# Moving two casts, one weight load, one transpose and two low parts in a mixed linear-attention and expert kernel

## The chip, the core and the metric

The kernel runs on one core of one Trainium2 chip. The metric is the device time of one execution in microseconds (us); lower is better. Engines are named as the profile names them: PE multiplies matrices, DVE, ACT and POOL work on tiles element by element, SP issues most DMAs. All work in their own order and wait for one another through semaphores.

## What is computed

Each of 2048 rows of x (512 wide) goes through two branches, and a gate mixes them.

```python
qkv = x @ wqkv                                    # q, k, v: 32 heads of 16
phi(a) = concat(softmax(a @ w_phi), softmax(-a @ w_phi))
kv, z  = sum_s phi(k) v, sum_s phi(k)             # over all rows
A = (phi(q) @ kv) / (phi(q) @ z + 1e-6) @ wo
q1, q2 = halves of x @ w_q                        # 32 heads
e = argmax(q1 @ k1.T) * 16 + argmax(q2 @ k2.T)    # one of 256 experts per head
B = sum over heads of gelu(x . u[e]) * v[e]
g = sigmoid(x . gate_w);  out = g * A + (1 - g) * B
```

## The kernel before

Rows are cut into 16 tiles of 128. To keep precision, an operand of a product is held as a high part (a cast, names ending in h) and a low part (the value minus the cast, names ending in l), and a product is three matmuls: high by high, high by low, low by high. A matmul over 512 columns is the unit in what follows.

**First phase (tiles 0 to 15).** Keys and values of a tile are projected, the softmaxes of the keys are made (`k_diffs` on DVE, `k_exp` on ACT, `k_sum` on DVE, `k_mult` on POOL), and `kvacc` adds the products with the values in one PSUM bank. From tile 5 on, tiles go in pairs (t, t+1) by a scheme that needs sums of the two tiles: `Sums.add` builds them on POOL, `Sums.high` casts them on ACT into `gh` (first sum) and the `xh` of tile 15's place (second sum), `Sums.low` subtracts on POOL into `gl` and `xl`. The products of a pair go into four rotating PSUM banks named pk, pu, pv and pk; a bank that is copied from another one is first written by ACT (L482: pu from pk), and pu of the next pair takes the bank of pv of this pair, which DVE's L549 reads last.

Beside this, the expert scores' weights are folded: `score` multiplies a piece of w_q (16 pieces, `load_wq` brings them into two buffers) with the keys k1, k2; `score_planes` (L297 on ACT, then a transposing DMA on SP) turns the result by way of 16-bit planes; `join_tp` and `join_end` (L308, L314 on ACT, L315 on POOL) put the planes together and split them into `sh`, `sl`. At t = 13 the query weights `rawq` come into one of the same two buffers, and PE folds them with w_phi (`foldq`, L208).

**Second phase (a = 0 to 15).** In step a the tile a is at the queries' softmax, b = a - 1 at turning and joining its planes, z = a - 2 at the output product. For tile z the products run: `mid_num` (L765, from `pt`, the joined planes of tile z's attention weights), the casts `xh` of its result (L769, ACT), the low parts `xl` (`num_lo`, L776, DVE), `back` (L877: 12 matmuls with `wo`'s parts; L884: 6 matmuls with `ch`, `cl`, the expert coefficients of the tile), `store`. The coefficients come from `count` (a chain of small bit operations on DVE, which `step` and `drain` deal out between other work; L800 to L824), `coef` (L828 on POOL), `c_planes` (L833 on ACT, a transposing DMA on SP), `c_join` (L840, L844 on ACT), `back_cl` (L865, DVE). `best` (L722, L723 on DVE) finds the best expert half by half, `turn_eq` sends its result through a transposing DMA on SP.

`wo` has four pieces. Pieces 2 and 3 are loaded together into one tile (`rawo2`, in the pool `late`); their high parts are made on ACT (L944, L973) and the low parts on POOL: piece 2 (`gl`) at L945 ahead of the loop, piece 3 (`wbl`) at L988 in step 1. After that `late` is closed (`cl_.close()` in step 1) and the pool `w4` is opened in the same memory; `pt` is its first tile, so the first `join` (L756) must wait until the last reader of `rawo2` has finished.

Nothing is scheduled automatically: each engine gets its instructions in the order in which the code issues them, and a wait holds up all that stands behind it on that engine. SP's DMAs are issued in order too.

Of the kernel before, what the change touches and what calls it, by code (L numbers as in the profile page):

```python
# [16 lines left out]
ALU = mybir.AluOpType  # L17
# [3 lines left out]
P = 128  # L21
S = 2048
D = 512
NT = S // P
# [11 lines left out]
def mix_kernel(ctx, tc, xT, wqT, wkT, wv, wphi, wo, wq, kk, ug, ev, cst, out):  # L36
# [103 lines left out]
    def stage(src, name, shape=None):  # L140
        t_ = wa_.tile(shape or [P, NK, D], F32, tag="st", bufs=2, name=name)
        if src is not None:
            sp.dma_start(t_, src)
        return t_
# [121 lines left out]
    def k_exp(t):  # L266
        act.activation(phis[t], phis[t], AF.Exp)  # L267
# [39 lines left out]
    def join_tp(j, tp, tj):  # L307
        act.copy(tj.bitcast(U16).rearrange("p (k n j) -> p j k n", j=2, n=P),  # L308
                 tp.rearrange("p (j k) n -> p j k n", j=2))

    def join_end(j, tj):
        js = slice(P * j, P * j + P)
        t3 = tj.rearrange("p (k e) -> p k e", k=NK)
        act.copy(sh[:, :, js], t3)  # L314
        pool.tensor_tensor(sl[:, :, js], t3, sh[:, :, js], op=ALU.subtract)  # L315

    st8 = {t: {} for t in range(NT)}

# [73 lines left out]
    def score(n, planes=True):  # L392
        nonlocal done
        for _ in range(n):
            score_w(done, raws[done])
            done += 1
            if done < 5:
                load_wq()
            if planes and done % 2 == 0:
                score_planes(done // 2 - 1)  # L400
# [63 lines left out]
    for t in range(5, NT - 1, 2):  # L464
# [53 lines left out]
        if behind:  # L518
            k_exp(behind)
            k_sum(behind)  # L520
            k_mult(behind)
        score(2, t > 5)
        if t > 5:
            load_wq()
            load_wq()
        if t == NT - 3:
            rawq = stage(wqT, "rawq")
        for u in (t - 3, t - 2):
            kvacc(u)
        vn, vt = v_tile(n), v_tile(t)  # L530
# [5 lines left out]
        d = pks[n] = mm_bank(f"pk{n}")  # L536
        act.copy(d, b)
        if t == 5:
            join_end(j2, tj2)
            score_planes(3)  # L540
            k_exp(t)
            x_low(9)
            k_sum(t)
            Sums.high(7, (0,))
            act.copy(vn, by16(e))
        prod(c, sums(1, 2), b22, False)
        if t == NT - 3:
            x_split(NT - 1)
        dve.tensor_tensor(vt, by16(c), vn, op=ALU.add)  # L549
# [1 line left out]
        o2 = d.rearrange("p (c n) -> p c n", c=2)  # L551
        prod(o2, tile_of(n, 2), b4, False)
        if t + 3 < NT:
            Sums.high(t + 2, (0, 1) if t > 5 else (1,))
            Sums.low(t + 2)
        if t == 7:
            for i in range(2):
                x_parts(i, 11)
# [383 lines left out]
        dve.tensor_tensor(zl[i], zsum[:, s_], zh[i], op=ALU.subtract)  # L942
    soft_exp(0)
    act.copy(woh[2], rawo[2])  # L944
    pool.tensor_tensor(wol[2], rawo[2], woh[2], op=ALU.subtract)  # L945
    front_s(1, 0)
    mid_mask(0)
    z_final(zh, zl)
# [12 lines left out]
    for a in range(NT - 1):  # L961
        n, b, z = a + 1, a - 1, a - 2
        owed = min(18, 3 * max(0, a - DEFER))
        left = min(18, 3 * max(0, a - DEFER + 1))
        B, Z = b >= 0, z >= 0
        if Z:
            mid_num(z)
        if a == 2:
            gelu_pre(a)
        if a == 1:  # L970
            front_q(a)
            v15 = vproj(NT - 1)
            act.copy(woh[3], rawo[3])  # L973
        if B:
            planes(b, 0)
            if Z:
                c_join(z)
            if a == 1:
                v15()
            planes(b, 1)  # L980
        if a > 1:
            front_q(a)
        if owed:
            back(z - 1, owed)
            store(z - 1)
        gelu_in(a)
        if a == 1:
            pool.tensor_tensor(wol[3], rawo[3], woh[3], op=ALU.subtract)  # L988
        if Z:
            num_lo(z)  # L990
        if B:
            if a == 1:
                for _ in gate(a):
                    pass
                soft_in(a)
                step(b, 6)
            else:
                soft_in(a, dealt(a, b, z))
                drain(b)
        else:  # L1000
            for _ in gate(a):
                pass
        if a != 1:
            gelu_act(a)
        if a > 0:
            soft_exp(a)
        if Z and not left:
            back(z)
            store(z)
        if not left and a > 1:  # L1010
            mid_mask(a)
        if a:
            front_s(n, 0)
        if left or a == 1:
            mid_mask(a)
            if 0 < left < 18:
                back(z, 18 - left)
        if a == 1:
            kvacc(NT - 1)
            kv_final()  # L1020
            cl_.close()
            w4 = ctx.enter_context(tc_pool("w4", "right"))
        front_s(n, 1)
        front_p(n, False)
        soft_w(a)
        if a == 1:
            best(n, 0)
        soft_sum(a, 0)
        soft_sum(a, 1)
        if a == 1:  # L1030
            drain(b)
        if a == 0:
            step(a, 6)
        if a != 1:
            best(n, 0)
        if a == 0:
            best(n, 1)
            turn_eq(n)
        soft_y(a, 0)
        soft_y(a, 1)  # L1040
        soft_p(a)
        if B:
            join(b)
            gelu_out(b)
            coef(b)
            c_planes(b)
            if a == 1:
                gelu_act(a)
        if a == 0:
            soft_b(a, lambda t: None)  # L1050
        else:
            soft_b(a)
            best(n, 1)
            turn_eq(n)
        if a != 1:
            gelu_pre(n)
# [123 lines left out]
```

## Time and profile before

| | |
|---|---|
| device time, median of 3 runs | 380.41 us (378.58 to 380.72) |
| the profiled execution: its own time | 380.69 us |
| its span, first to last instruction | 378.9 us |
| mean granted clock of PE | 0.991 |
| busy: PE, DVE, ACT, POOL | 97%, 89%, 68%, 54% of the span |

A row of the timeline reads: start in us from the span's first instruction, duration in us, engine, line, operation, output and inputs, shapes, count; then, in brackets, how long the engine sat idle before it and which instruction ended that. A row of windows gives, for a stretch of time, how long each engine was busy (with the number of instructions), and then the mean clock that PE was granted (1.00 is full), the share of DMA time and GB/s.

### The profile page before, as it was taken

The numbers are of one execution on the slowest core, as the hardware profiler recorded it, in microseconds if no ns is written. First come the engines' busy times: TensorE is split into PE (matmuls) and PEld (weight loads), VectorE is DVE, ScalarE is ACT, GpSimd is POOL, SyncE is SP. The second block draws the span as 40 slices with busy tenths as digits, with TensorE's granted clock in tenths as the row PEclk, the third lists the DMA queues.
The fourth block names the chain that finished last, engine by engine and source line by source line (L and its number), as shares of the span: only waits on it lengthen the run. The fifth ranks groups of instructions, "written<-read, shape, count | busy, mean of one in ns | idle before, by whom it ended". The sixth has DMA issues, their size and how long they took to land.

```text
span 378.9 us, 8840 instructions
## 1 busy us (share of the span) xinstructions
PE 367.3 (97%) x3443; PEld 288.0 (76%) x3443; DVE 335.8 (89%) x785; ACT 256.7 (68%) x459; POOL 205.0 (54%) x206
## 2 busy tenths in 40 slices
PE   7999999999999999699999999999999999999995
PEld 4766766877777878578888888888788888888875
DVE  4679999989695989999999999999999999999993
ACT  5576678776554775478768677686696687687741
POOL 1089989978658565336427336344454464364700
PEclk9999999999998999989999999999999999999999
DMA  7867997656852306143361441441643523623501
GB/s 274 325 243 243 285 285 176 213 143 261 304 153 76 84 4 67 20 97 78 77 99 50 104 97 45 83 102 37 113 45 82 126 54 73 126 52 75 69 33 55
DMA packets 72074, 46.67 MB, mean 123 GB/s; under 512 B 63584, under 2 KB 64480, under 8 KB 69728
## 3 DMA queue, kind: packets, MB, share of 16 engines
q1 hardware_dynamic: 71168, 45.24, 45.9%
q10 hardware_dynamic: 864, 0.87, 0.8%
q8 instruction: 27, 0.44, 0.5%
q14 instruction: 15, 0.12, 0.1%
HBM read 26.43 MB, written 4.19 MB: 81 GB/s over the span
## 4 chain that ended last, share of the span: by engine, by line
PE 78%; DVE 9%; POOL 4%; ACT 3%; issue 3%; DMA 2%; POOLq 0%; ACTq 0%
PE po L877 11%; PE s L56 6%; PE s L57 6%; PE s L58 6%; PE pk L454 5%; PE po L884 5%; PE pu L454 4%; PE ws L292 4%; PE pq L56 4%; PE pq L58 3%; PE pq L57 3%; PE oT L765 2%; PE kvacc L283 2%; PE pe L454 2%; PE pv L454 2%
## 5 line engine op out<-in xcount | busy, mean ns | idle before, releaser
L679 POOL TENSOR_TENSOR w<-d,zb 128x512 f32<-128x512 f32 x32 | 41.1, 1302 | 76.1 <-ACT d L673 76.1
L56 PE MATMUL s<-sh,xh 128*128 128x512 f32 x128 | 51.6, 403 | 0.0
L58 PE MATMUL s<-sh,xl 128*128 128x512 f32 x128 | 50.5, 395 | 0.0
L57 PE MATMUL s<-sl,xh 128*128 128x512 f32 x128 | 50.4, 394 | 0.0
L714 POOL TENSOR_TENSOR d<-d,st 128x512 f32<-128x512 f32 x30 | 31.2, 1062 | 30.9 <-DVE st L708 26.6
L673 ACT ACTIVATE d<-d 128x512 f32<-128x512 f32 x32 | 20.0, 632 | 34.0 <-DVE d L119 25.9
L276 POOL TENSOR_TENSOR d<-d,st 128x1024 f32<-128x1024 f32 x16 | 32.5, 2032 | 9.8 <-ACT d L267 7.9
L756 ACT COPY pt<-tp 128x1024 uint16<-128x1024 uint16 x28 | 36.3, 1368 | 0.0
L746 ACT COPY pl<-d 128x1024 uint16<-128x1024 uint16 x28 | 29.2, 1044 | 6.5 <-POOL d L714 6.4
L58 PEld LDWEIGHTS s<-sh,xl 128*128 128x128 f32 x128 | 24.4, 191 | 5.2
L57 PEld LDWEIGHTS s<-sl,xh 128*128 128x128 f32 x128 | 24.5, 191 | 4.8
L56 PEld LDWEIGHTS s<-sh,xh 128*128 128x128 f32 x128 | 24.4, 190 | 4.8
L56 PE MATMUL pq<-wah,xh 128*128 128x512 f32 x64 | 26.8, 418 | 0.0
L58 PE MATMUL pq<-wah,xl 128*128 128x512 f32 x64 | 25.1, 392 | 0.0
L57 PE MATMUL pq<-wal,xh 128*128 128x512 f32 x64 | 25.0, 390 | 0.0
L723 DVE TENSOR_TENSOR eq<-s,mx 128x512 bf16<-128x512 f32 x32 | 22.1, 692 | 1.1
L683 DVE TENSOR_REDUCE st<-d 128x32 f32<-128x512 f32 x32 | 21.6, 681 | 1.4
L722 DVE TENSOR_REDUCE mx<-s 128x32 f32<-128x512 f32 x32 | 21.8, 680 | 0.0
L156 DVE TENSOR_TENSOR xl<-xr,xh 128x512 fp32r<-128x512 f32 (+2 forms) x17 | 20.2, 1204 | 1.7 <-ACT xh L152 1.6
L271 DVE TENSOR_REDUCE st<-d 128x64 f32<-128x1024 f32 x16 | 19.4, 1215 | 2.1 <-ACT d L267 1.8
L693 DVE TENSOR_REDUCE st<-w 128x32 f32<-128x512 f32 x32 | 20.4, 676 | 0.1
L267 ACT ACTIVATE d<-d 128x1024 f32<-128x1024 f32 x16 | 17.1, 1066 | 4.1 <-DVE d L121 4.1
(272 smaller groups left out, 1126.5 us busy)
## 6 DMA issues: line engine op xcount, KB each, us to landing
wq<-wq SPq DMA_DIRECT2D x16, 1024.0 KB, 6.1
xr<-xT SPq DMA_DIRECT2D x15, 256.0 KB, 5.3
y<-ot SPq DMA_DIRECT2D x15, 256.0 KB, 2.3
rawk<-wkT SPq DMA_DIRECT2D x1, 1024.0 KB, 6.1
rawq<-wqT SPq DMA_DIRECT2D x1, 1024.0 KB, 5.4
rawu<-ug SPq DMA_DIRECT2D x2, 258.0 KB, 5.7
rawv<-wv ACTq DMA_DIRECT2D x2, 256.0 KB, 4.5
rawv<-wv SPq DMA_DIRECT2D x2, 256.0 KB, 5.5
```

What stands on the lines that cost most here:

```text
L56: pe.matmul(o, ah, bh, start=(first and i == 0), stop=False)
L57: pe.matmul(o, ah, bl, start=False, stop=False)
L58: pe.matmul(o, al, bh, start=False, stop=(last and i == n - 1))
L276: pool.tensor_tensor(g64(d), g64(d), b64(st[:, 128:192]), op=ALU.mult)
L454: pe.matmul(o, x_, w_, start=(first and i + j == 0), stop=(i == 1 and j == 2), skip_group_check=True)
L679: pool.tensor_tensor(hs(e["w"], i), hs(e["ph"], i), hs(zb, i), op=ALU.mult)
L714: eng.tensor_tensor(g64(d)[:, gs_], g64(d)[:, gs_], r[:, gs_].unsqueeze(2).to_broadcast([P, 32, F]), op=ALU.mult)
L722: dve.tensor_reduce(mx, p3, axis=AX.X, op=ALU.max)
L723: dve.tensor_tensor(e["eq"][:, 512 * half:512 * half + 512].rearrange("p (h f) -> p h f", f=F), p3, mx.unsqueeze(2).to_broadcast([P, H, F] ...
L746: act.copy(pl, e["ph"][:, halves[i]].bitcast(U16).rearrange("p (c j) -> p j c", j=2))
L756: act.copy(p16[:, :, 4 * i:4 * i + 4, :], e["tp"][i].rearrange("p (j g) n -> p j g n", j=2))
L877: pe.matmul(po, a, b, start=(i == 0), stop=False)
```

## The change

Five things are moved; PE's own order stays as it was. (1) At t = 5, ACT casts the first sum of the pair 7, 8 ahead of the exponentials of tile 5, and the second ahead of the copy of tile 6's values; POOL makes both low parts ahead of the low part of the joined scores. (2) At t = 13, the DMA of `rawq` is issued ahead of the transposing DMA of the last scores. (3) Tile 0's coefficient planes (`c_planes(0)`) are made in step 2 behind the casts of tile 0's numerators, no longer in step 1. (4) Piece 2 of `wo` gets its low part in step 0 behind `soft_w`, and piece 3 gets it on DVE, behind `drain(0)` in step 1. (5) Step 0 deals out five of `count`'s pieces for tile 0, not six; the sixth (L800, L802) goes to step 1.

```diff
+    def join_high(j, tj):
+        act.copy(sh[:, :, P * j:P * j + P], tj.rearrange("p (k e) -> p k e", k=NK))
+
+    def join_low(j, tj):
+        js = slice(P * j, P * j + P)
+        pool.tensor_tensor(sl[:, :, js], tj.rearrange("p (k e) -> p k e", k=NK), sh[:, :, js], op=ALU.subtract)
+
     def join_end(j, tj):
...
+        join_high(j, tj)
+        join_low(j, tj)
...
-        score(2, t > 5)
-        if t > 5:
+        score(2, 5 < t < NT - 3)
+        if t == NT - 3:
+            rawq = stage(wqT, "rawq")
+            score_planes(7)
+        elif t > 5:
             load_wq()
             load_wq()
-        if t == NT - 3:
-            rawq = stage(wqT, "rawq")
...
         if t == 5:
-            join_end(j2, tj2)
+            join_high(j2, tj2)
             score_planes(3)
+            Sums.high(7, (0,))
             k_exp(t)
             x_low(9)
             k_sum(t)
-            Sums.high(7, (0,))
+        prod(c, sums(1, 2), b22, False)
+        if t == 5:
+            Sums.high(7, (1,))
             act.copy(vn, by16(e))
-        prod(c, sums(1, 2), b22, False)
...
         if t + 3 < NT:
-            Sums.high(t + 2, (0, 1) if t > 5 else (1,))
+            if t > 5:
+                Sums.high(t + 2)
             Sums.low(t + 2)
+            if t == 5:
+                join_low(j2, tj2)
...
     act.copy(woh[2], rawo[2])
-    pool.tensor_tensor(wol[2], rawo[2], woh[2], op=ALU.subtract)
...
         if a == 2:
+            c_planes(z)
             gelu_pre(a)
...
-        if a == 1:
-            pool.tensor_tensor(wol[3], rawo[3], woh[3], op=ALU.subtract)
...
         if a == 1:
             drain(b)
+            dve.tensor_tensor(wol[3], rawo[3], woh[3], op=ALU.subtract)
         if a == 0:
-            step(a, 6)
+            pool.tensor_tensor(wol[2], rawo[2], woh[2], op=ALU.subtract)
+            step(a, 5)
...
             coef(b)
-            c_planes(b)
             if a == 1:
                 gelu_act(a)
+            else:
+                c_planes(b)
```

Lines of the changed program have other numbers than those of before; the names of the tiles tell which is which. On ACT at t = 5, from the copy into pk of tile 6 to the copy into pu of tile 7, before (xr_397 and xr_359 are the two sums of the pair 7, 8, d_635 tile 5's differences, v_714 tile 6's values):

```order
L537 COPY pk_724<-pu_589 128x512 [waits PE_49]
L314 CAST sh<-wtj_627 128x4x128 [waits Activation_49]
L297 COPY wpl_728<-ws_641 128x1024
L267 ACTIVATE d_635<-d_635 128x1024 [waits DVE_49]
L183 CAST gh<-xr_397 128x512 [waits Pool_49]
L545 COPY v_714<-pe_607 128x32x16
L183 CAST xh_67<-xr_359 128x512 [waits PE_49,Pool_49]
L152 CAST xh_65<-xr_579 128x512 [waits DMAHW5_49]
L482 COPY pu_775<-pk_768 128x512 [waits DVE_49,PE_49]
```

and in the changed program:

```order
L543 COPY pk_724<-pu_589 128x512 [waits PE_49]
L312 CAST sh<-wtj_627 128x4x128 [waits Activation_49]
L297 COPY wpl_727<-ws_641 128x1024
L183 CAST gh<-xr_397 128x512 [waits Pool_49]
L267 ACTIVATE d_635<-d_635 128x1024 [waits DVE_49]
L183 CAST xh_67<-xr_359 128x512 [waits PE_49,Pool_49]
L554 COPY v_714<-pe_607 128x32x16
L152 CAST xh_65<-xr_579 128x512 [waits DMAHW5_49]
L487 COPY pu_775<-pk_768 128x512 [waits DVE_49,PE_49]
```

The cast into gh now stands ahead of the exponentials of tile 5, and the cast into xh_67 ahead of tile 6's values; the copy into pu_775 at the end still waits for DVE.

On ACT in steps 1 and 2, from the copies that join tile 0's planes (pt) to the casts of tile 0's numerators (oT) and the first work of tile 2 (pp), before:

```order
L756 COPY pt_2062<-tp_0_1930 128x2x512 [waits DMAHW3_49,Pool_49]
L756 COPY pt_2062<-tp_0_1935 128x2x512 [waits DMAHW4_49]
L833 COPY plc_2067<-cf_2057 128x512 [waits Pool_49]
L645 ACTIVATE gs_1892<-gs_1892 128x1
L646 ACTIVATE x_1896<-x_1896 128x256
L647 ACTIVATE x_1896<-x_1896,gs_1892 128x256 [waits Activation_49]
L769 CAST xh_65<-oT_0_2091 128x256 [waits PE_49]
L769 CAST xh_65<-oT_0_2092 128x256 [waits PE_49]
L619 ACTIVATE gs_2111<-pp_2031 128x1
```

and in the changed program:

```order
L767 COPY pt_2062<-tp_0_1926 128x2x512 [waits DMAHW3_49,DVE_49,Activation_49]
L767 COPY pt_2062<-tp_0_1931 128x2x512 [waits DMAHW4_49]
L656 ACTIVATE gs_1888<-gs_1888 128x1
L657 ACTIVATE x_1892<-x_1892 128x256 [waits Pool_49]
L658 ACTIVATE x_1892<-x_1892,gs_1888 128x256 [waits Activation_49]
L780 CAST xh_65<-oT_0_2087 128x256 [waits PE_49]
L780 CAST xh_65<-oT_0_2088 128x256 [waits PE_49]
L844 COPY plc_2107<-cf_2056 128x512 [waits Pool_49]
L630 ACTIVATE gs_2111<-pp_2029 128x1
```

The copy of the coefficient planes (plc) has gone behind the casts of the numerators, and the first joining copy, which waited for POOL (`rawo2`'s last reader, L988), now waits for DVE, where that last reader stands.

On SP in the same steps, one piece of the difference (et_2085 and et_2089 are the transposed result of `best(2)`, tpc the coefficient planes of tile 0, tp_1 the planes of tile 1), before:

```order
L729 DMA_TRANSPOSE et_1880<-eq_1873 128x8x128
L748 DMA_TRANSPOSE tp_0_1930<-pl_0_1928 128x8x128
L748 DMA_TRANSPOSE tp_0_1935<-pl_0_1933 128x8x128
L835 DMA_TRANSPOSE tpc_2069<-plc_2067 128x4x128
L729 DMA_TRANSPOSE et_2089<-eq_2047 128x8x128
L748 DMA_TRANSPOSE tp_1_2121<-pl_1_2119 128x8x128
```

and in the changed program:

```order
L740 DMA_TRANSPOSE et_1876<-eq_1869 128x8x128
L759 DMA_TRANSPOSE tp_0_1926<-pl_0_1924 128x8x128
L759 DMA_TRANSPOSE tp_0_1931<-pl_0_1929 128x8x128
L740 DMA_TRANSPOSE et_2085<-eq_2045 128x8x128
L846 DMA_TRANSPOSE tpc_2109<-plc_2107 128x4x128
L759 DMA_TRANSPOSE tp_1_2121<-pl_1_2119 128x8x128
```

The transposing DMA of tile 0's coefficient planes has gone behind that of `best(2)`.

More of the change, by code (lines that the diff above doesn't have):

```diff
@@ L309, in join_tp @@
                  tp.rearrange("p (j k) n -> p j k n", j=2))
+    def join_high(j, tj):
[3 more added lines that the diff above has]
+        pool.tensor_tensor(sl[:, :, js], tj.rearrange("p (k e) -> p k e", k=NK), sh[:, :, js], op=ALU.subtract)
     def join_end(j, tj):
[L312 to L315, printed above, removed]
+        join_high(j, tj)
+        join_low(j, tj)
     st8 = {t: {} for t in range(NT)}
```

## The prediction

> **What bounds the kernel now.** I read the page's first part, then PE's own timeline for its idle time, then the stretches with the granted clock, and last the timelines of the engines that end PE's waits.
>
> ```profile
> PE 367.3 (97%) x3443; PEld 288.0 (76%) x3443; DVE 335.8 (89%) x785; ACT 256.7 (68%) x459; POOL 205.0 (54%) x206
> ```
>
> PE is busy for 97% of the span, and the change leaves PE's instructions and their order alone. So time can change only where PE waits or where its clock is low. Three waits stand out in its timeline:
>
> ```profile
> 60.09 0.39 PE L454 MATMUL pe<-t1l,gh 128*128 128x512 f32 x1
> 61.41 0.50 PE L454 MATMUL pe<-t1h,gl 128*128 128x512 f32 x1 [0.93 <-POOL gl L189]
> 62.45 0.39 PE L454 MATMUL pu<-uh,xh 128*128 128x512 f32 x1
> ...
> 113.26 0.39 PE L58 MATMUL pk<-wah,xl 128*128 128x512 f32 x1
> 114.37 2.06 PE L208 MATMUL foldq<-wp,rawq 32*128 32x32 f32 x64 [0.72 <-DMA rawq<-wqT]
> ...
> 154.95 0.50 PE L56 MATMUL pq<-wah,xh 128*128 128x512 f32 x1
> 161.66 0.80 PE L877 MATMUL po<-t1h,xh 128*128 128x512 f32 x1 [3.69 <-ACT xh L769]
> ```
>
> Successive matmuls start 0.23 apart. Measured so, the waits lose 1.1 us (60.09 to 61.41, less 0.23), 0.8 to 0.9 us (113.26 to 114.37) and 3.9 us. Now the clock, in stretches of 3.41 us:
>
> ```profile
> 113.60:117.01 3.41, 2.69 (x68) 2.51 (x68) 2.25 (x4) 2.46 (x3) 2.80 (x5) 1.00 0.28 99
> 117.02:120.43 3.41, 3.41 (x10) 2.64 (x9) 2.73 (x5) 1.48 (x3) 2.84 (x2) 0.50 0.35 120
> 120.43:123.84 3.41, 3.41 (x189) 3.01 (x190) 0.33 (x1) 0.94 (x2) 2.82 (x3) 1.00 0.00 0
> 157.98:161.39 3.41, 0.00 (x0) 0.00 (x0) 3.38 (x16) 1.78 (x5) 0.72 (x1) 1.00 0.00 0
> 161.39:164.80 3.41, 3.14 (x7) 2.48 (x8) 3.34 (x10) 3.34 (x9) 2.78 (x3) 0.50 0.46 104
> ```
>
> The first number behind the length is PE's busy time, the 1.00 or 0.50 is its clock. After the second and after the third wait comes one stretch at half clock, which loses 3.41 / 2 = 1.7 us if PE is busy in it. The change aims at all three waits. I take them in turn; line numbers are those of before.
>
> **A: casts of the sums at t = 5, worth +0.1 us.**
>
> ```profile
> 57.87 1.08 ACT L267 ACTIVATE d<-d 128x1024 f32<-128x1024 f32 x1
> 58.83 0.62 ACT L183 CAST gh<-xr 128x512 fp32r<-128x512 f32 x1
> 59.34 0.60 ACT L545 COPY v<-pe 128x512 f32<-128x512 f32 x1
> 61.42 0.57 ACT L482 COPY pu<-pk 128x512 f32<-128x512 f32 x1 [0.45 <-DVE v L549]
> ...
> 58.98 1.22 DVE L271 TENSOR_REDUCE st<-d 128x64 f32<-128x1024 f32 x1
> 60.70 0.63 DVE L549 TENSOR_TENSOR v<-pv,v 128x512 f32<-128x512 f32 x1
> ...
> 58.49 1.63 POOL L315 TENSOR_TENSOR sl<-wtj,sh 128x512 fp32r<-128x512 f32 x1
> 60.08 1.27 POOL L189 TENSOR_TENSOR gl<-xr,gh 128x512 fp32r<-128x512 f32 x1
> ```
>
> With `gh` cast at 57.87, POOL makes `gl` in the place of the scores' low part, from 58.49 to about 60.1, before PE asks for it at 60.3. That wait goes. But the cast takes 0.51 (58.83 to 59.34) of ACT ahead of the exponentials, which then run from 58.4 to 59.5. DVE's sum, which starts 0.03 behind them, comes at 59.5 for 58.98, L549 at 61.2 for 60.70, and ACT's copy into pu, which waits for L549, ends at 62.5. PE comes to the first matmul on pu at 61.2 now, stands there for 1.3 us, and starts it at 62.55; before it was 62.45. One wait is swapped for another. Bounds: -1.1 if DVE did not matter, +0.2 if the new one costs a little more. POOL's next work is reordered but has the same end.
>
> **B: `rawq` ahead of the transpose, worth -2.4 us.**
>
> ```profile
> 103.57 1.92 PE L292 MATMUL ws<-wq,kp 128*32 128x512 f32 x16
> ...
> 106.60 2.22 SPq L299 DMA_TRANSPOSE wtp<-wpl  x1
> 108.93 0.51 SPq L143 DMA_DIRECT2D rawq<-wqT  x1
> ...
> rawq<-wqT SPq DMA_DIRECT2D x1, 1024.0 KB, 5.4
> ...
> 120.89 1.99 PE L208 MATMUL foldq<-wp,rawq 32*128 32x32 f32 x64
> 126.48 2.54 POOL L594 TENSOR_TENSOR t1l<-rawo,t1h 128x512 fp32r<-128x512 f32 x2 [3.23 <-ACT t1h L593]
> ```
>
> The buffer of `rawq` is free when the first half of the ws matmuls has ended, near 104.5. Issued then, it lands near 110 after its 5.4 us, while PE wants it at 113.6. Even 3 us of delay would be harmless. The transpose behind it waits for ACT until 106.6 anyway and is read at 115.5, so both orders serve it. The fold starts at 113.6 for 114.37: 0.8 us.
>
> The larger part is the clock. The 64 small matmuls of the fold with the wait beside them were followed by half clock; the second fold (120.89), in a stretch without a wait, was not. Without the wait the first fold looks like the second, with 1.4 us of full matmuls beside it in any stretch, so I expect full clock: 1.7 us less (1.6 after rounding of the starts). What follows moves along: the casts of the fold's result, then L594, before which POOL sat idle 3.2 us, then `zsum`, then DVE's work of step 0. None of these waits for something that stays late. Bounds: -2.5, and -0.7 if half clock stays.
>
> **C: step 0 to 2, worth +0.9 us.** I work at the old clock times and let B move all of it.
>
> ```profile
> 138.93 0.73 DVE L800 TENSOR_TENSOR m<-sa 128x64 uint16<-128x64 uint16 x1
> 140.79 0.68 DVE L722 TENSOR_REDUCE mx<-s 128x32 f32<-128x512 f32 x1
> 149.41 1.27 DVE L813 TENSOR_SCALAR T<-X 128x256 uint32<-128x256 uint32 x1
> 157.06 0.28 DVE L818 TENSOR_TENSOR T<-X 128x256 uint16<-128x256 uint16 x1
> 158.56 1.27 DVE L693 TENSOR_REDUCE st<-w 128x32 f32<-128x512 f32 x2
> 162.06 0.69 DVE L723 TENSOR_TENSOR eq<-s,mx 128x512 bf16<-128x512 f32 x1
> ...
> 149.05 1.48 POOL L988 TENSOR_TENSOR wbl<-rawo,wbh 128x512 fp32r<-128x512 f32 x1
> ...
> 151.91 2.60 ACT L756 COPY pt<-tp 128x1024 uint16<-128x1024 uint16 x2
> 159.55 0.62 ACT L833 COPY plc<-cf 128x512 uint16<-128x512 uint16 x1 [5.03 <-POOL cf L828]
> 164.03 0.77 ACT L840 COPY ctj<-tpc 128x512 uint16<-128x512 uint16 x1
> 164.82 0.41 ACT L844 CAST ch<-ctj 128x256 fp32r<-128x256 f32 x1
> ...
> 165.97 0.39 PE L884 MATMUL po<-eh,ch 128*128 128x512 f32 x1
> ```
>
> DVE first. Without L800 and L802 in step 0 its next work (140.79) starts at 138.93, 1.9 us earlier, and keeps this until step 1's differences end, near 146.6. There the small steps of tile 0's count follow. L813 and its neighbours took about 1.3 us each beside POOL's L988 and its successors; with L988 gone POOL pauses, five steps run in 2.1 us, and the two that still meet POOL's pair of products end with it, near 151.4. Half of `best` and two sums follow (2.5 us, to 153.9), then the last six steps: five took 1.5 us (157.06 to 158.56), the sixth 0.5. The count ends near 155.8, 2.8 us earlier than 158.6, and the new low part of `wo`'s last piece (0.7 us, like L723) at 156.5.
>
> Here is the new wait. `pt` lies where `rawo2` lay, so ACT's first joining copy waits for that low part: 156.55 for 151.91, and the pair of copies ends at 159.15. PE needs `pt` for tile 0's numerators; its projection, at 154.95 before, starts 0.4 us behind the copies (as 154.95 behind 154.5), at 159.55. So PE's wait is not removed but comes ahead of `pq`, and is 5 us long. Queued behind the joining copy on ACT are the casts `xh` and the planes `plc`; PE waits for both.
>
> Then `ch`. SP now issues the transpose of `best(2)` first, and that waits for DVE's L723: it ended 4.2 us after the L693 of 158.56 started, so now at 156.45 + 4.2 = 160.65. Its issue takes 1.2 us, the coefficients' transpose lands 2.3 us after its own (the next rows), and L840, L844 take 1.2 us: 165.6. PE gets there from 159.55 by 12 matmuls of pq and 12 of po, 2.8 + 2.7 us: 165.1. So `ch` would be last, and its matmul would start 0.35 us earlier than 165.97.
>
> What decides is the clock: 5 us without work are followed by half clock. With the stretches of this execution, moved by 2.3 us, PE's idle time fills most of two, 153.4 to 156.9 and 156.9 to 160.3. The first costs 0.4 us until 160.3, the second, if it counts, another 1.7; 0.5 of it lies beside the wait for `ch`. So C is -0.35 (0.4 is covered by the wait for `ch`) or 0.4 + 1.7 - 0.5 - 0.35 = +1.25. I take +0.9, nearer to the second, since the stretch at 113.60 had 2.69 us of busy PE and was still followed by 0.50. Stretches may fall otherwise in other executions, and the values between are then possible.
>
> [...]
>
> **Sum.** +0.1 - 2.4 + 0.9 = -1.4 us against the profiled execution's 380.69: 379.3. The median shown is 0.28 lower, so **379.0 us** on its scale. A difference of 0.5% (1.9 us) is about what a measurement of this kernel can tell from no change.
>
> **Rivals.**
>
> ```profile
> DMA to landing us min/median/max: 2.3/2.3/4.5
> ```
>
> 1. The change does all it says: no wait at pu, and tile 0's output runs without one. For it speaks that each wait's named cause is moved away; against it L482's wait for L549 and `pt`'s place. A -1.1, B -2.4, C -3.9: 373.0. Chance 0.04.
> 2. Only one slow stretch in step 2: C is -0.35, the sum -2.7, so 377.8. Speaks for it that the second stretch holds some matmuls. Chance 0.22.
> 3. Half clock stays after the fold: B is -0.7, the sum +0.3: 380.7. Against it the second fold. Chance 0.10.
> 4. Slower: the coefficients' transpose, now behind another one on SP, lands after 4.5 us, the longest of the 14 above, not after 2.3. `ch` then comes at 167.8, PE stands idle for 2.7 us more, and a further slow stretch costs 1.4: C is +3.3, the sum +1.0: 381.4. It decides from a landing of about 2.9 us on; most landings were 2.3. Chance 0.10.
>
> The forecast keeps 0.54. **Range.** From A at nothing with B and C at their lower ends, -2.9, to B at -0.7 with C at +1.25 and A at +0.2, +0.8: 377.5 to 381.2; this leaves out the first rival and half of the fourth. Faster by over 0.5% (below 378.5) are rivals 1 and 2 and a part of the forecast: 0.36. Slower by over 0.5% (above 382.3) needs the fourth with a slow fold: 0.09. The rest, 0.55, is within.
>
> **What would show it.** A: PE without a wait before `gl`, but with about 1 us ahead of pu, ended by ACT's copy. B: `rawq` issued near 104.5, no wait before the fold, clock 1.00 in the stretch behind it. C: ACT's first joining copy ended by DVE's new subtraction near 154 on the new clock, PE waiting ahead of `mid_num`, then little before `po<-eh,ch`, and one or two stretches at 0.50. Wrong would be: PE runs through `mid_num` without a wait (`pt` is free earlier), or waits long before `ch` (SP's order costs more), or half clock after the fold.

## The result, and the profile after

The changed kernel takes **380.43 us** (median of 12 executions, 378.72 to 381.33), the kernel before 380.21 us (12 executions, 378.10 to 381.83): ratio **1.0007**, 95% interval 0.9985 to 1.0030. The change makes no difference that can be measured. The profiled execution took 380.58 us, with a span of 378.8 us.

The engines' busy times hardly move. The page's first part of the changed kernel:

```profile
PE 367.2 (97%) x3443; PEld 288.5 (76%) x3443; DVE 333.3 (88%) x786; ACT 256.5 (68%) x459; POOL 204.9 (54%) x205
```

PE's timeline of the changed kernel, at the three places of the prediction:

```profile
61.17 0.40 PE L459 MATMUL pe<-t1h,gl 128*128 128x512 f32 x1
62.72 0.50 PE L459 MATMUL pu<-uh,xh 128*128 128x512 f32 x1 [1.15 <-ACT pu L487]
...
113.65 0.39 PE L58 MATMUL pk<-wah,xl 128*128 128x512 f32 x1
113.97 1.99 PE L208 MATMUL foldq<-wp,rawq 32*128 32x32 f32 x64
...
151.86 0.29 PE L58 MATMUL pp<-uh,xl 128*128 128x258 f32 x1
156.24 0.45 PE L776 MATMUL oT<-pt,kvb 64*32 64x128 f32 x16 [4.10 <-ACT pt L767]
157.44 0.68 PE L776 MATMUL oT<-pt,kvb 64*32 64x128 f32 x16 [0.75 <-ACT gs L656]
158.05 0.79 PE L56 MATMUL pq<-wah,xh 128*128 128x512 f32 x1
...
166.26 0.39 PE L895 MATMUL po<-eh,ch 128*128 128x512 f32 x1
```

The wait for `gl` is gone and one of 1.15 stands ahead of pu. The fold starts without a wait. Then PE stands 4.10 us ahead of tile 0's numerators, and 0.75 us between their halves, where nothing stood before; ahead of `po<-t1h,xh` and of `po<-eh,ch` it does not wait. The row names ACT's `gs` for the second half; by the order of the work it is the second joining copy, which ends there (below).

The stretches of 3.41 us of the changed kernel, two at the fold and four in steps 1 and 2 (length, PE's busy time first, then the granted clock):

```profile
112.50:115.91 3.41, 3.41 (x72) 2.84 (x70) 2.37 (x4) 1.77 (x5) 3.41 (x5) 1.00 0.23 64
115.91:119.33 3.42, 3.42 (x36) 2.65 (x32) 3.30 (x5) 2.97 (x5) 2.24 (x3) 1.00 0.42 134
...
153.46:156.87 3.41, 0.45 (x16) 0.18 (x16) 3.38 (x12) 2.01 (x2) 1.02 (x1) 1.00 0.00 0
156.87:160.29 3.42, 2.85 (x21) 2.04 (x22) 2.67 (x9) 3.33 (x11) 2.08 (x2) 0.50 0.06 16
160.29:163.70 3.41, 3.41 (x9) 2.64 (x8) 0.12 (x1) 2.54 (x5) 0.73 (x1) 0.50 0.67 145
163.70:167.11 3.41, 3.41 (x16) 2.80 (x15) 3.27 (x11) 2.09 (x5) 0.00 (x0) 1.00 0.55 103
```

The fold keeps the full clock. Behind the new wait come two stretches at 0.50, where before had one at each place. Last, what PE waits for, in the timelines of DVE, ACT and SP of the changed kernel:

```profile
153.75 0.42 DVE L835 TENSOR_TENSOR cf<-X 128x256 f32<-128x256 uint8 x1
154.09 0.68 DVE L1041 TENSOR_TENSOR wbl<-rawo,wbh 128x512 fp32r<-128x512 f32 x1
...
154.86 2.53 ACT L767 COPY pt<-tp 128x1024 uint16<-128x1024 uint16 x2 [6.00 <-issue]
158.95 0.63 ACT L844 COPY plc<-cf 128x512 uint16<-128x512 uint16 x1
163.42 0.40 ACT L855 CAST ch<-ctj 128x256 fp32r<-128x256 f32 x1
...
158.92 1.23 SPq L740 DMA_TRANSPOSE et<-eq  x1
160.25 1.21 SPq L846 DMA_TRANSPOSE tpc<-plc  x1
```

ACT sits idle 6.00 us and starts joining `pt` as soon as DVE's new low part `wbl` has ended: the wait that the prediction drew.

PE's starts at the same instruction, changed kernel less before, show the two big terms against each other (each start counted from the span's first instruction):

| PE comes to | before | after | difference |
|---|---|---|---|
| first fold of the queries | 114.37 | 113.97 | -0.40 |
| second fold of the queries | 120.89 | 118.83 | -2.06 |
| first product of tile 0's output, `po<-t1h,xh` | 161.66 | 163.34 | +1.68 |
| mk of tile 2 | 167.33 | 167.62 | +0.29 |

In this pair of executions 2.1 us are gained at the folds, and all of it is given back in steps 1 and 2. So the question for the experiments was: is the gain at the folds real, is the loss real, and what makes each of them?

### The profile page after: what moved, and what is told of

Read it like the earlier page. It is cut to its first block, busy times and chain, and to the rows that moved or that the text cites. A ratio compares the mean times of both kernels' runs of the same rounds, so it can differ in the third digit from the quotient of the medians.

```text
span 378.8 us, 8837 instructions
## 1 busy us (share of the span) xinstructions
PE 367.2 (97%) x3443; PEld 288.5 (76%) x3443; DVE 333.3 (88%) x786; ACT 256.5 (68%) x459; POOL 204.9 (54%) x205
## 4 chain that ended last, share of the span: by engine, by line
PE 83%; issue 5%; DVE 4%; POOL 3%; ACT 3%; DMA 1%; SPq 0%; POOLq 0%; ACTq 0%; DVEq 0%
PE po L888 11%; PE s L56 6%; PE s L57 6%; PE s L58 6%; PE po L895 5%; PE pq L56 4%; PE pk L459 4%; PE pu L459 4%; PE ws L292 4%; PE pq L58 4%; PE pq L57 4%; PE oT L776 3%; PE kvacc L283 2%; PE pp L57 2%; PE pp L58 2%
## 5 line engine op out<-in xcount | busy, mean ns | idle before, releaser
L56 PE MATMUL s<-sh,xh 128*128 128x512 f32 x128 | 50.8, 397 | 0.0
L56 PE MATMUL pq<-wah,xh 128*128 128x512 f32 x64 | 27.8, 434 | 0.0
L58 PE MATMUL pq<-wah,xl 128*128 128x512 f32 x64 | 26.0, 406 | 0.0
L57 PE MATMUL pq<-wal,xh 128*128 128x512 f32 x64 | 25.9, 405 | 0.0
```

Source lines behind the costliest of these rows:

```text
L56: pe.matmul(o, ah, bh, start=(first and i == 0), stop=False)
L57: pe.matmul(o, ah, bl, start=False, stop=False)
L58: pe.matmul(o, al, bh, start=False, stop=(last and i == n - 1))
```

## How half clock is counted

The granted clock of an execution tells how many stretches it spent at half: one stretch of 3.41 us lowers the mean over 379 us by 0.0045, so 0.995 is one, 0.991 two, 0.986 three. The profiled execution of before, at 0.991, is at half clock for 3.41 us twice, from 117.02 to 120.43 and from 161.39 to 164.80, and between them at full clock for 40.96 us, 12 times as long; that of the changed kernel, also at 0.991, is at half clock for 6.83 us at once, from 156.87 to 163.70. Every timed execution has such a figure. The executions of the kernel before in all the comparisons below (96, one with 0.945 left out):

| stretches at half clock | 0 | 1 | 2 | 3 |
|---|---|---|---|---|
| before: executions | 3 | 46 | 35 | 11 |
| before: mean us | 378.2 | 379.4 | 380.3 | 382.0 |
| after: executions | 0 | 3 | 9 | 0 |
| after: mean us | | 379.2 | 380.5 | |

The same kernel takes 378 or 382 us with this number, and at the same number before and after take the same time within 0.2 us. On average the changed kernel has 1.75 such stretches, before 1.57; with 12 executions of the changed kernel this difference is not clear of noise.

## The experiments

Experiments 1 to 3 make the parts of the change apart, on the kernel before: part 2, part 1, and parts 3 to 5 together.

**e1: part 2 alone** (the diff's hunk with `rawq = stage(...)` and `score_planes(7)`).

> Before with part 2 of the change alone (rawq's DMA ahead of the transpose). Theory (the gain of B is real and was given back by C): no wait before the first fold, clock 1.00 behind it, and all that follows 2.4 us earlier, so 377.8 beside before's 380.2, ratio 0.9937; the wait before tile 0's output (3.9 us in before) stays as it is. Rival (the 2.4 us that PE gains at the folds are lost again at tile 0's output whatever steps 0 to 2 do, because the chain that ends in the casts xh of tile 0's numerators does not move along): PE is 2.4 us early at the second fold, its wait before po<-t1h,xh grows by as much, ratio 1.000.

Measured: 379.41 us (377.81 to 380.64, apart from one stray execution of 1001 us), ratio to before 0.9981, interval 0.9957 to 1.0005. Neither: a third of the forecast. The interval reaches from 1.6 us faster to 0.2 us slower, so the forecast of 2.4 us lies outside it, while no gain at all lies within. Its stretches around tile 0's output:

```profile
156.53:159.94 3.41, 0.36 (x2) 0.00 (x0) 3.31 (x14) 1.44 (x4) 0.72 (x1) 1.00 0.00 0
159.94:163.36 3.42, 2.78 (x7) 2.20 (x8) 3.35 (x12) 3.33 (x10) 2.77 (x3) 0.50 0.32 73
163.36:166.77 3.41, 3.41 (x10) 2.64 (x9) 3.23 (x9) 2.71 (x6) 0.00 (x0) 0.50 0.73 146
```

PE's wait there is the old one (156.51 to 160.58), but the stretch without work ends 0.64 us before PE goes on, not 0.27 us as in before (161.39, 161.66). The half-clocked stretch then holds 2.78 us of work, not 3.14, and a second one follows. Seven of its executions have two stretches, four one: 1.64 on average, no fewer than before. So part 2 takes away a wait, but in these executions not, on average, a stretch at half clock.

**e2: part 1 alone** (the hunks at t = 5).

> Before with part 1 of the change alone (the casts of the sums at t = 5). Theory (one wait swapped for another): the wait of 0.93 before pe<-t1h,gl goes, one of about 1.3 us comes before the first matmul on pu, ended by ACT's copy into pu, which waits for DVE's v; sum +0.1 to +0.3 us, ratio 1.0005. Rival (the wait for gl goes and nothing takes its place): 1.1 us less, ratio 0.997.

Measured: 379.82 us, ratio 0.9998 (0.9974 to 1.0022). PE's timeline has the theory's wait (61.41 to 62.98, 1.18 us idle, ended by ACT's pu), and the rival's 0.997 lies outside the interval, if narrowly.

**e3: parts 3, 4 and 5 alone** (the hunks from `act.copy(woh[2], rawo[2])` on).

> Before with parts 3, 4 and 5 of the change alone (coefficient planes, low parts of wo, count's sixth piece). Theory: PE waits 4 to 5 us ahead of tile 0's numerators, for the copy into pt that waits for DVE's new low part, and two stretches at half clock follow; 2.0 to 2.4 us slower, 382.4, ratio 1.006. The half clock behind the first fold stays as in before. Rival (these parts cost nothing by themselves, and the loss in the changed kernel comes only from PE reaching tile 0's output 2.4 us earlier than it is served): PE's waits in steps 1 and 2 together are no longer than before's 3.9 us and one stretch is at half clock; ratio 1.000.

Measured: 380.47 us, ratio 1.0022 (0.9999 to 1.0045), that is +0.8 us: less than the theory's 2.0 to 2.4, and the rival's 1.000 is at the interval's edge. The waits are those of the theory (4.08 ahead of the numerators). What failed is my sentence on the fold, whose wait this kernel keeps:

```profile
111.10:114.51 3.41, 2.78 (x13) 1.96 (x11) 3.38 (x6) 1.86 (x5) 3.41 (x3) 1.00 0.91 359
114.51:117.93 3.42, 3.40 (x70) 3.15 (x71) 2.26 (x4) 3.16 (x4) 2.24 (x5) 1.00 0.32 95
```

```profile
114.53 0.74 PE L208 MATMUL foldq<-wp,rawq 32*128 32x32 f32 x17 [0.65 <-DMA rawq<-wqT]
```

Two stretches of e3, and the fold in PE's timeline: the wait falls into one stretch and the fold into the next, since a stretch, counted in steps of 3.41 us, happened to begin at 114.51. Behind the stretch with the wait the clock stays at 1.00, though nothing at the fold was changed. In the profiled execution of before both lay in 113.60 to 117.01. This was the first hint that the half clock behind the fold belongs to how the stretches lie in an execution, not to the kernel.

**e4: the new wait taken away.** On the changed kernel:

```
                 soft_in(a)
+                dve.tensor_tensor(wol[3], rawo[3], woh[3], op=ALU.subtract)
                 step(b, 6)
...
             drain(b)
-            dve.tensor_tensor(wol[3], rawo[3], woh[3], op=ALU.subtract)
```

> The changed kernel with one edit: DVE's low part of wo's piece 3 stands at the start of step 1's queries (behind soft_in), ahead of the last bit operations of tile 0's count, not behind them. Theory: the wait of 4.3 us ahead of tile 0's numerators goes, since pt's place is free early; PE then stands before po<-eh,ch instead, since the transpose of the coefficient planes is issued behind the one of best(2) as in the changed kernel and ch comes near 163.8: PE passes there at about 164, 2.3 us earlier than 166.3, and about half of this is lost to one more stretch at half clock behind it. 379.2 beside the changed kernel's 380.4, ratio to before 0.997 (0.994 to 0.9985). Rival (the wait ahead of the numerators is the only price, and ch follows the numerators wherever they are): no wait left in step 2, no half clock, 6 us less than the changed kernel: 374.5, ratio 0.985.

Measured: 380.63 us, ratio 1.0012 (0.9990 to 1.0035). Neither. The wait ahead of the numerators is gone (they start at 152.02, straight behind 151.80), and two others take its place:

```profile
159.50 0.73 PE L888 MATMUL po<-t1h,xl 128*128 128x512 f32 x2 [2.06 <-DVE xl L787]
164.10 0.80 PE L895 MATMUL po<-eh,ch 128*128 128x512 f32 x1 [3.40 <-ACT ch L855]
```

Its stretches there:

```profile
157.84:161.26 3.42, 1.19 (x4) 0.67 (x4) 3.32 (x10) 1.08 (x2) 2.70 (x3) 1.00 0.32 73
161.26:164.67 3.41, 0.57 (x1) 0.50 (x2) 1.55 (x5) 1.79 (x3) 0.00 (x0) 0.50 0.59 119
164.67:168.08 3.41, 3.41 (x16) 2.41 (x15) 3.24 (x10) 1.96 (x5) 0.13 (x1) 0.50 0.40 77
```

PE passes `ch` at 164.1 as the theory said, 2.2 us earlier than 166.26. But this is lost again at half clock: the stretch from 164.67 to 168.08 runs at 0.50, where the changed kernel is at full clock from 163.70 on. Each of the 12 executions has two stretches at half clock; I had let only half of the gain go there. An earlier time at one place of PE is worth nothing if the stretches at half clock move with it.

**e5: `ch` ahead.** On e4, SP's transpose of the coefficient planes ahead of that of `best(2)`:

```
         if a == 2:
             c_planes(z)
+            turn_eq(a)
             gelu_pre(a)
+            c_join(z)
...
-            if Z:
+            if Z and a > 2:
                 c_join(z)
...
             best(n, 1)
-            turn_eq(n)
+            if a != 1:
+                turn_eq(n)
```

> The kernel of e4 with the transpose of tile 0's coefficient planes issued on SP ahead of that of best(2), and ch made on ACT ahead of the planes of tile 1. Theory (in e4 and in the changed kernel ch comes last through SP's order): the planes are ready near 156.6, their transpose lands near 159.0, ch is there near 160.2 and PE passes po<-eh,ch near 160.5 for 164.1 in e4; the wait of 2.2 us for xl stays, and a stretch or two at half clock with it. Some 3 us less than e4's 380.6: 377.5, ratio to before 0.993 (0.989 to 0.997). Rival (what PE gains there is lost again to a later bound, the transposed best(2) or DVE): no more than 1 us less than e4, ratio 0.998 or more.

Measured: 377.04 us (376.29 to 378.33), ratio **0.9927** (0.9904 to 0.9951): the theory's number.

```profile
157.17 1.19 SPq L846 DMA_TRANSPOSE tpc<-plc  x1
159.72 1.23 SPq L740 DMA_TRANSPOSE et<-eq  x1
...
160.08 0.73 PE L888 MATMUL po<-t1h,xl 128*128 128x512 f32 x2 [2.03 <-DVE xl L787]
161.11 0.40 PE L895 MATMUL po<-eh,ch 128*128 128x512 f32 x1
163.25 0.73 PE L895 MATMUL po<-eh,cl 128*128 128x512 f32 x2 [1.06 <-DVE cl L876]
```

The stretch with the longest wait and the next one:

```profile
156.57:159.98 3.41, 1.48 (x7) 0.90 (x5) 3.38 (x16) 2.26 (x7) 1.64 (x2) 1.00 0.17 38
159.98:163.40 3.42, 2.25 (x9) 1.57 (x10) 3.28 (x12) 3.36 (x7) 1.14 (x2) 1.00 0.49 107
```

The transpose is issued at 157.17 for 160.25 in the changed kernel, and PE goes through `ch` without a wait. The waits that are left, for `xl` and `cl`, bring no half clock in this execution, nor in three more of the six. So in e4 `ch` was held by SP's order: there ACT had the planes ready at 156.57 and SP issued their transpose only at 160.48. In the changed kernel the planes are themselves late. ACT copies them behind the joining copies and the casts of the numerators, until 158.95 + 0.63 = 159.58, and SP issues their transpose at 160.25, so that SP's order costs 0.7 us there at most; PE came later still and did not notice.

**e6: the wait filled.** On the changed kernel, in `mid_num`:

```
+        if t == 0:
+            for _ in range(18):
+                pe.matmul(o[0], wah[:, 0, 0:P], wah[:, 0, :], start=True, stop=True, skip_group_check=True)
         for g in range(8):
```

> The changed kernel with 18 matmuls added that nothing needs, 128x512 each, on PE just ahead of tile 0's numerators, where PE stands for 4.3 us; they write a bank that the numerators then overwrite. They keep PE busy for 4.1 us and remove no wait. Theory (of what steps 0 to 2 give back, the half clock is the larger part): PE starts the numerators at the same 156.2, but pq's 12 matmuls take 2.8 us for 5.3, PE stands 0.1 us for ch at 163.8 and comes to mk of tile 2 near 165.4 for 167.6. 2.2 us less than the changed kernel's 380.4: 378.2, ratio to before 0.995 (0.993 to 0.997). Rival (the wait itself is the price; what comes after, ch above all, holds PE until the same time at any clock): within 0.5 us of the changed kernel, ratio to before 1.000.

Measured: 379.02 us, ratio to before 0.9984 (0.9965 to 1.0004). The theory gave 2.2 us less than the changed kernel and the rival none; measured are 1.4 us by the medians and 0.9 us by the two ratios to before (0.9984 and 1.0007), and the interval does not rule out the rival. What speaks against the rival is the clock and the profile. All 12 executions have a granted clock of 0.999 or 1.000. In its profile the theory's steps are met: counted from the fold of the keys, PE comes to mk of tile 2 2.3 us earlier than in the changed kernel. The wait is as long as ever, so what was gained is the clock's part of its price; e9 and e10 below measure that part side by side.

**e7: work in PE's order.** On e4: in step 1 `drain(b)` ahead of `best(n, 0)`; `mid_num`, `num_lo`, `c_planes`, `c_join` of tile 0 moved to the end of step 1, ahead of `soft_b`, and `back_cl` behind it; in step 2 `mid_mask(a)` behind `front_s(n, 0)`.

```
+            drain(b)
             best(n, 0)
...
                 gelu_act(a)
+                mid_num(b)
+                num_lo(b)
+            c_planes(b)
+            if a == 1:
+                c_join(b)
...
             soft_b(a)
+            if a == 1:
+                back_cl(b)
             best(n, 1)
```

> The kernel of e4 with the work of step 1 and 2 put in the order in which PE wants it: on DVE the rest of tile 0's count ahead of best(2)'s first half, and the low parts xl of tile 0's numerators and cl of its coefficients ahead of best(2)'s second half; on SP the coefficients' transpose ahead of best(2)'s; on ACT ch ahead of tile 1's planes; on PE the mask of tile 2 behind the first half of the scores of tile 3. Theory (all of the loss is such waits and the half clock behind them): PE runs from tile 0's numerators through po<-eh,ch and cl with less than 1.5 us of waiting and no stretch at half clock; the limit is then DVE, which sat idle 4.3 us between 153 and 167.6 in the changed kernel. 5 us less than before: 375.2, ratio 0.987 (0.983 to 0.991). Rival (DVE, busy for 96% from step 8 on, sets the end, and PE's gain is lost in waits for it): ratio 0.996 or more, with new waits of PE after 250 us.

Measured: 377.01 us (376.28 to 378.33), ratio 0.9930 (0.9906 to 0.9953), between the two and the same as e5. Tile 0's output runs without a wait and no execution has half clock, but PE now comes too early for what follows:

```profile
164.92 0.36 PE L795 MATMUL mk<-wm,et 128*128 128x16 bf16 x8 [0.55 <-DMA et<-eq]
169.24 0.36 PE L56 MATMUL pp<-uh,xh 128*128 128x258 f32 x1 [1.12 <-DVE d L121]
171.54 0.45 PE L776 MATMUL oT<-pt,kvb 64*32 64x128 f32 x16 [0.62 <-ACT pt L767]
172.74 0.45 PE L776 MATMUL oT<-pt,kvb 64*32 64x128 f32 x16 [0.75 <-ACT pt L767]
```

Some of PE's gain is lost in later waits, as the rival said, but not where it put them, and mostly not to DVE: 3 us go at once, 0.55 to the transposed `best(2)`, 1.12 to the bank that DVE's differences of tile 2 free and 1.37 to the planes of tile 1, and there is no new wait after 250 us.

**e8: part 1's wait taken away.** On e7:

```
             Sums.high(7, (0,))
-            k_exp(t)
-            x_low(9)
-            k_sum(t)
-        prod(c, sums(1, 2), b22, False)
+            act.copy(vn, by16(e))
+            x_low(9)
+        prod(c, sums(1, 2), b22, False)
         if t == 5:
             Sums.high(7, (1,))
-            act.copy(vn, by16(e))
...
         dve.tensor_tensor(vn, by16(b), vn, op=ALU.add)
+        if t == 5:
+            k_exp(t)
+            k_sum(t)
```

> The kernel of e7 with one more edit at t = 5: ACT copies tile 6's values ahead of the exponentials of tile 5, and DVE adds both tiles' values ahead of the sum of tile 5's exponentials. Theory (the wait that part 1 brought before the first matmul on pu comes from DVE's order): the wait of 1.3 us goes, nothing takes its place, and all that follows is 1.1 us earlier: ratio to e7 0.997, to before 0.984. Rival (a third wait takes its place, the exponentials being late for the products of the keys): the same time as e7.

Measured: **375.62 us** (375.30 to 375.75), ratio to before **0.9885** (0.9863 to 0.9907); to e7 0.9963, as the theory had it (the level in front of it, e7's, was higher than expected). The wait ahead of pu is gone, and nothing takes its place:

```profile
61.54 0.40 PE L459 MATMUL pe<-t1h,gl 128*128 128x512 f32 x1
62.06 0.50 PE L459 MATMUL pu<-uh,xh 128*128 128x512 f32 x1
```

This kernel beats both, by 1.2%.

**e9 and e10: what the clock follows.** PE's busy time in a stretch does not tell the clock of the next one: before's stretch from 113.60 with 2.69 us is followed by 0.50, e5's from 156.57 with 1.48 us by 1.00. Of the 2.69 us most is the fold, whose matmuls use 32 of PE's 128 rows (`32*128`, 2.06 us). So the theory was that the rows count. Two fillings of the same wait test this: e6 with `wah[0:32, 0, ...]` (32 rows) or `wah[0:64, 0, ...]` (64 rows) as both operands. The theory gave half clock in nearly every execution for 32 rows, 380.4 to 382 us, and a granted clock of 0.999 to 1.000 for 64 rows, 379.0 us.

> As e6, but the 18 added matmuls use 32 of PE's 128 rows (they sum over 32 rows, not 128); they last as long and move as many columns. [...] Rival (the clock follows PE's busy time): clock 1.00 in nearly every execution and 379.0, as in e6.

> As e6, but the 18 added matmuls use 64 of PE's 128 rows. [...] Rival (any use of less than all rows leads to half clock, or PE has to be busy with full products): half clock as in e9.

Measured: e9 380.70 us, ratio to before 1.0023 (0.9998 to 1.0047), one or two stretches at half clock in each of 11 executions; e10 378.62 us, ratio 0.9969 (0.9941 to 0.9996), 0.998 or more in each of 11. PE's row of the added matmuls and the stretches that they fill, first of e9:

```profile
152.41 4.40 PE L775 MATMUL oT<-wah 32*128 32x512 f32 x18
```

```profile
153.20:156.61 3.41, 3.41 (x16) 2.56 (x14) 3.27 (x12) 1.42 (x2) 1.03 (x1) 1.00 0.02 5
156.61:160.02 3.41, 3.02 (x37) 1.77 (x37) 3.29 (x13) 3.34 (x8) 2.08 (x2) 0.50 0.00 0
```

And of e10:

```profile
153.75 4.37 PE L775 MATMUL oT<-wah 64*128 64x512 f32 x18
```

```profile
151.69:155.10 3.41, 3.41 (x21) 2.92 (x21) 3.24 (x8) 0.00 (x0) 0.28 (x1) 1.00 0.00 0
155.10:158.51 3.41, 3.39 (x30) 2.29 (x28) 3.37 (x12) 1.98 (x2) 1.03 (x1) 1.00 0.02 5
```

e9's stretch from 153.20, in which PE is busy with 32 rows for 3.41 us, is followed by 0.50; e10's from 155.10, in which it is busy with 64 rows for 3.39 us, is followed by 1.00 (156.41 to 159.82). Both rivals fall. The two kernels differ in nothing but the rows that the added matmuls use, these last equally long (4.40 and 4.37 us), and both were timed side by side: between them lie 2.1 us, and their intervals do not overlap. So half clock behind the new wait costs about 2 us, near the 2.2 us that e6's theory gave. That the rows count is shown for this wait; how much work in a stretch keeps the clock full is not.

**e11 and e12: part 2 by itself.** Before, and e1, each with 16 such matmuls (128 rows) ahead of the first product of `back(0)`, so that half clock can come only behind the fold:

```
+        if t == 0:
+            for _ in range(16):
+                pe.matmul(po, wah[:, 0, 0:P], wah[:, 0, cols], start=True, stop=True, skip_group_check=True)
         for i, (a, b) in enumerate(mms):
             pe.matmul(po, a, b, start=(i == 0), stop=False)
```

> Before with 16 added matmuls, 128x512, in front of po<-t1h,xh of tile 0, where PE stands for 3.85 us; nothing needs them, and the first product overwrites their bank. So half clock can come only behind the first fold. [...] Theory of the prediction (the half clock behind the first fold belongs to the kernel before): mean granted clock 0.995 in all executions. Theory now (it belongs to the phase of the stretches): 0.995 in about 4 of 10, 1.000 in the others; time about 378.3, ratio to before 0.9955.

> The kernel of e1 (part 2 alone) with the same 16 added matmuls: no wait before the first fold and none to bring half clock later. Granted clock 1.000 in every execution. Against e11 it shows what part 2 is worth by itself. Theory of the prediction: 2.4 us, ratio of the two 0.9937. Theory now: 0.8 us of waiting and 1.7 us in 4 of 10 executions, together 1.5 us, ratio 0.996.

Measured: e11 378.75 us, ratio to before 0.9968 (0.9946 to 0.9989), with one stretch at half clock in 2 of 12 executions; e12 378.05 us, ratio 0.9955 (0.9935 to 0.9975), with none in 12. Between the two medians lie 0.7 us, a ratio of 0.998 (between the means 0.5 us); by the width of the two intervals this cannot be told from nothing, but it is less than 2.4 us. The prediction's theory falls: in ten of twelve executions the fold's wait brings no half clock. Of the other profiles that keep the old order at the fold, before has 0.50 behind the stretch of the wait and e3 1.00. The 4 of 10 of my theory of then, and with it the 1.5 us, was an estimate that no run shows; measured are 2 of 12, which do not rule it out, and 0.7 us. One reason stands in e11's profile: in this execution PE comes to the fold 0.5 us later than in before (its last matmul starts at 113.76, not 113.26), the DMA does not, and the wait is 0.24 us instead of 0.72.

```profile
114.39 2.06 PE L208 MATMUL foldq<-wp,rawq 32*128 32x32 f32 x64 [0.24 <-DMA rawq<-wqT]
```

## Why the prediction came out as it did

The forecast was 379.0 us, the measured time is 380.43: inside the range, and "no difference" was given the largest chance. The mechanisms were drawn rightly, one term was not. That the time fell inside the range is owed to its width: its upper end let the fold keep half clock, which did not happen, and the sum itself was 1.4 us too low.

| step, us | forecast | profiled pair, PE's starts counted from the fold of the keys | that part alone, over executions |
|---|---|---|---|
| A, casts of the sums | +0.1 | +0.1 | -0.1 (e2: 0.9974 to 1.0022) |
| B, `rawq` ahead | -2.4 | -2.3 | -0.7 (e1: 0.9957 to 1.0005; e12 against e11: -0.7) |
| C, steps 0 to 2 | +0.9 | +2.4 | +0.8 (e3: 0.9999 to 1.0045) |
| sum | -1.4 | +0.1 | 0.0 |

- **A** was right in each step: no wait ahead of `gl`, about 1.2 us ahead of pu, ended by ACT's copy behind DVE's L557. e8 took the wait away by another order of the values' copy on ACT and of the sums on DVE, which bears out that this order is the cause.
- **B failed in its size**, in the step "I expect full clock: 1.7 us less". That the changed fold keeps the full clock was right. But that before loses 1.7 us there was read from one execution, and it is so in 2 of 12 (e11). The argument that led there, that the wait beside the fold is followed by half clock, left out how the stretches lie: before's from 113.60 holds both and is followed by 0.50; in e3 a boundary, at 114.51, lies between them, and the clock stays at 1.00. In the profiled pair 2.3 us are there; over executions about 0.7 are left, the size of the wait alone.
- **C was right in its mechanism**: ACT's first joining copy at 154.86, right behind DVE's low part (2.1 us more on the old clock, 157.0; the forecast had 156.55), PE standing ahead of the numerators, no more wait ahead of `po<-t1h,xh`, `ch` at 163.8, its transpose issued right behind that of `best(2)`. In the profiled pair it cost more than forecast: PE's pq began 0.6 us later than worked out (158.05 and 2.1 for 159.55), and both stretches at half clock lay in its work (pq's 12 matmuls took 163.34 - 158.05 = 5.3 us for 2.8), where I had let 0.4 us of the first count. Over executions +0.8 is close to +0.9, but as the mean of a term that jumps from execution to execution, for which the forecast had only a sentence and no share in the sum.
- The third rival, half clock staying after the fold, gave 380.7, nearest to the measured time, by a cause that did not occur: no execution with part 2 and a filled wait (e12) shows it.
- The stretches do not begin at the same time in each profile: at 113.60 in before, at 112.50 in the changed kernel, at 114.51 in e3. So the 1.7 us should have stood in the sum as a term with a chance.

So where did the gain go? By the medians the wait for `rawq` was worth about 0.7 us, and the new wait for DVE's low part costs about as much; neither is clear of noise by itself. The kernel before has none to three stretches at half clock, the changed one has one or two, 1.57 and 1.75 on average, and the changed one loses no less there.

## What to carry to other kernels

Before a stretch at half clock is put into a sum, look whether it is in every execution: the mean granted clock of each tells how many it had, and one profile shows only one. A wait can cost its length and half clock behind it, here about 2 us (e9 against e10), so filling it with products that nothing needs shows which of them is paid. When the last reader of a buffer is moved to another engine, look up what is next put into that memory: here a subtraction of 0.68 us, queued on DVE behind the count, held up a copy, a projection and a product.

## What the runs showed of the hardware

**The clock.** Followed by half clock were these stretches at full clock, with PE's busy time in them: before's from 157.98 with 0.00 us, e1's from 156.53 with 0.36, the changed kernel's from 153.46 with 0.45, e4's from 157.84 with 1.19, before's from 113.60 with 2.69, of which the fold on 32 rows takes 2.06, and e9's from 153.20 with 3.41 on 32 rows. Followed by full clock were e5's from 156.57 with 1.48 and e10's from 155.10 with 3.39. Of the stretches at half clock, before's from 161.39 with 3.14 us and the changed kernel's from 160.29 with 3.41 were followed by full clock, and e4's from 161.26 with 0.57, e1's from 159.94 with 2.78, the changed kernel's from 156.87 with 2.85 and e9's from 156.61 with 3.02 by another at half. Of what decides this, e9 and e10 alone set one thing on purpose, the rows.

**DVE and POOL.** Executions of one kernel without any half clock still lie in two groups 1.5 us apart (e6: seven from 378.31 to 379.09, five from 380.23 to 380.30). The traces show a difference of that size. Near 110 us DVE's `xl` and POOL's product start within 0.1 us of each other, and one of the two takes long: in before and the changed kernel POOL's takes 2.47 and 2.50 us and `xl` 0.69, in e1 and e7 POOL's takes 1.94 us and `xl` 2.40 and 2.47. First before, then e1:

```profile
110.08 0.69 DVE L156 TENSOR_TENSOR xl<-xr,xh 128x512 fp32r<-128x512 f32 x1 [0.23 <-ACT xh L152]
...
110.10 2.47 POOL L276 TENSOR_TENSOR d<-d,st 128x1024 f32<-128x1024 f32 x1
```

```profile
110.00 2.40 DVE L156 TENSOR_TENSOR xl<-xr,xh 128x512 fp32r<-128x512 f32 x1 [0.23 <-ACT xh L152]
...
109.92 1.94 POOL L276 TENSOR_TENSOR d<-d,st 128x1024 f32<-128x1024 f32 x1
...
112.46 0.50 PE L58 MATMUL pk<-wah,xl 128*128 128x512 f32 x1 [1.16 <-DVE xl L156]
```

In e1, where POOL is 0.08 us ahead, `xl` takes 2.40 us and ends 0.54 us behind POOL's product, and PE, which needs it, stands 1.16 us; in before POOL takes 2.47 us and PE does not wait. In e7 and the changed kernel the rows' starts lie 0.02 us apart or less, too close to tell who came first. e7's profile (378.33 us), which has no half clock and a long `xl`, is an execution of the upper group of its kernel (378.32 and 378.33; the other four from 376.28 to 377.13). That this is what parts the two groups agrees with that one profile, but no run set it on purpose.
